# Attention into a top-1 mixture of experts: half of the first weights, the second layer's and two stores moved behind the gathered rows, plan steps spread over the next block

## The chip, the core and the metric

The kernel runs on one core of a Trainium2 chip. The core has five engines with queues of their own: TensorE (PE, products and transposes; PEld is its weight load), VectorE (DVE), ScalarE (ACT), GpSimd (POOL) and SyncE (SP, which here only issues DMAs). They wait for one another by semaphores. The metric is the device time of one execution in microseconds, as the median of several runs.

## The reference

Two stages. First a chunked attention: 4 batches, 8 heads, 768 positions, head size 64; each chunk of 32 positions sees 16 positions to its left, 8 to its right and 8 memory slots. Its output x has 3072 tokens of 512 numbers. Then each token goes to one of eight experts:

```python
logits = x @ w_gate + modality_bias[modality_id]
e_idx = np.argmax(logits, axis=1)
gate_w = probs[np.arange(N), e_idx]     # probs: softmax of the logits
for e in range(E):
    mask = e_idx == e
    h = np.maximum(x[mask] @ w1[e], 0.0)      # 512 -> 1024
    out[mask] = gate_w[mask, None] * (h @ w2[e])   # 1024 -> 512
```

All is in fp32; the kernel splits the expert products into a rounded high part and a low part (the difference), so that each product of the reference is three on TensorE.

## The kernel before, in words

**Attention.** 16 units (a batch and two heads), two halves each, in one long loop. After each unit its output (tile xb) is stored to a DRAM tensor xd, whose rows are tokens: 512 numbers of x and 16 copies of the gate. After each batch, route(b) computes the logits, the expert of each token, its place in the expert's list, and the gates; it is a generator whose steps third() and pump() put between other work. The list of tokens of each expert is a table of columns.

**Expert blocks.** Work then goes in slots, each with a block of up to 256 tokens of one expert. gather(row) reads the block's token numbers from the table (a column whose number stands in a register), and two indirect DMAs on GpSimd's queue fetch 128 rows of xd each into xg[0] and xg[1]. load_w(row, half) issues on SP eight loads of 256 KB: half 0 is the first layer (raw[0] to raw[7]), half 1 the second (raw[8] to raw[15]); they are skipped by a register if the block has the expert of the one before. cast makes the high parts on ScalarE; less makes the low parts on VectorE or GpSimd; conv is both. trans transposes the gathered rows and splits them (xt); mm1(f) makes one of eight pieces of the hidden layer (12 products), after which ScalarE and VectorE write its high and low part (h); mm2(f) makes the second layer's products for both halves of the tokens.

**The passage.** Block 0 is of the expert that is largest after three batches, and takes tokens of those alone. So its weights are loaded and its rows gathered while batch 3's attention ends, and mm1 and mm2 of block 0 run beside batch 3's routing. When that is done, plan_early finds block 1 (register regs1), and plan_rest, another generator, finds all the others (register regs). In the first slot (opening) plan_rest's steps stand between other work on VectorE, and what is left is run at its end; the slot after it begins with its loads and its gather, which need regs, and then the stores of block 0's results.

**What sets the order.** Each engine runs its instructions in program order, and so do SP's and GpSimd's DMA issues: a DMA that waits holds all that are behind it. A load into a buffer waits for the last reader of that buffer. In a slot, TensorE runs eight mm1 of the block, then mm2(0) to mm2(2), trans(0) of the next block, mm2(3), trans(1), and the rest of mm2. Results of transposes and of mm1 go through four buffers in turn (bank, named tr).

The functions that the diff touches, with the lines of the profile:

Of the kernel before, what the change touches and what calls it, by code (L numbers as in the profile page):

```python
# [20 lines left out]
P = 128  # L21
# [12 lines left out]
HEAD = 3  # L34
# [14 lines left out]
def tile_chunk_attention_top1_moe(  # L49
# [344 lines left out]
    def trans_x(u, hf):  # L394
        b, g = divmod(u, 4)
        xb = xbs[u]
        t = bank()
        for i in range(3):
            nc.tensor.transpose(t[:, i * P:(i + 1) * P], xb[:, 3 * hf + i, :], ident)
        if hf == 0:  # L400
            xTs[u] = rt.tile([P, S], F32, name="xT", bufs=5)
        nc.scalar.copy(xTs[u][:, 384 * hf:384 * hf + 384], t[:, 0:384])
        if hf == 1:
            (nc.sync if u in (NU - 4, NU - 3) else nc.gpsimd).dma_start(xd[b * S:(b + 1) * S, g * P:(g + 1) * P].rearrange("(t p) c -> p t c", p=P), xb)


    routing, now = [], [0]
# [165 lines left out]
    def route(b):  # L573
# [86 lines left out]
        yield "v"  # L660
        nc.vector.reciprocal(sx, sx)
        yield "v"
        gt = sm.tile([P, NT, XW - DM], F32, name="gt")
        nc.gpsimd.tensor_copy(gt, sx.to_broadcast([P, NT, XW - DM]))
        with nc.allow_non_contiguous_dma(reason="one gate per token"):
            (nc.sync if b == B - 2 else nc.gpsimd).dma_start(xd[b * S:(b + 1) * S, DM:XW].rearrange("(t p) c -> p t c", p=P), gt)
        if b == B - 2:

            nc.vector.reduce_max(cm, cb, axis=AX.X)
# [15 lines left out]
        for t in range(NT):  # L685
            if b != B - 2 or t not in early:
                yield from one_hot(b, t, lo, ac, hot)
        yield "late" if b < B - 1 else "pe"
        tb = bank()
        for t, (l1, a1) in enumerate(hot):  # L690
# [20 lines left out]
    gate_now, gate_out = [const.tile([P, 2], F32, name=f"gate_{i}") for i in range(2)]  # L711
    ev = {}

    def load_w(row, half):
        if half == 0:
            if row == 0:
                ev[0] = nc.values_load(regs0[0:1, 0:1], engines=[mybir.EngineType.SP], min_val=0, max_val=E - 1,
                                       skip_runtime_bounds_check_because="the place of one of 8 experts")
            else:
                r = (regs1 if row < 2 else regs)[row:row + 1]  # L720
                ev[row] = nc.values_load(r[:, 0:1], engines=[mybir.EngineType.SP], min_val=0, max_val=E - 1,
                                         skip_runtime_bounds_check_because="the place of one of 8 experts, or 0")
                ev[row, "c"] = nc.values_load(r[:, 1:2], engines=[mybir.EngineType.SP], min_val=0, max_val=1,
                                              skip_runtime_bounds_check_because="a comparison gives 0 or 1")
        e = ev[row]
        kw = {} if row == 0 or row == ROW_X and half == 0 else {"cond": ev[row, "c"]}
        for f in range(8):
            if half == 0 and row < ROW_X:
                nc.sync.dma_start(
                    raw[f].rearrange("p (c f) -> p c f", f=P),  # L730
                    w1[ds(e, 1), :, f * P:(f + 1) * P].rearrange("o (c p) f -> p (o c) f", p=P), **kw)
            elif half == 0:
                src = w1[ds(e, 1), :, (f // 4) * DM:(f // 4 + 1) * DM]
                c = f % 4
                nc.sync.dma_start(
                    raw1[32 * c:32 * c + 32, f - c:f - c + 4],
                    src[:, c * P:(c + 1) * P].rearrange("o (c s) f -> s (o c) f", s=32), **kw)
            else:
                nc.sync.dma_start(raw[8 + f], w2[ds(e, 1), f * P:(f + 1) * P, :].rearrange("o p d -> p (o d)"), **kw)
# [176 lines left out]
    for i in range(n + 1):  # L916
        live = i < n
        u, hf = units[i] if live else (NU, 0)
        now[0] = i
        if i == MAN:  # L920
            man.enter_context(tc.manual_schedule(engines={mybir.EngineType.Pool}))
        if i < n - 1:
            scores(u, hf)
        if 1 <= i < n - 1:
            exps_t(*units[i - 1])
        if i == n - 5:
            third(7)
        if i < n - 1:
            less_max(u, hf)
            if i == 1:  # L930
                nc.vector.memset(vws[1][0:64, :, D:2 * D], 0.0)
            pump(1)
        if u + 1 < NU and hf == 0:
            trans_k(u + 1)
            regroup_q(u + 1)
            pump(3)
            store_k(u + 1, 1, 0, nc.scalar.copy)
            store_k(u + 1, 0, 0, nc.scalar.copy)
            store_k(u + 1, 0, 1, nc.scalar.copy)
            store_k(u + 1, 1, 1, nc.scalar.copy)  # L940
            pump(3)
        elif u + 1 < NU:
            if u == 0:
                nc.gpsimd.iota(iota_i, [[1, 192]], base=0, channel_multiplier=0)
                mem_keys(2, nc.gpsimd)
            if 0 < u < NU - 2:
                mem_keys(u + 2, nc.gpsimd)
            if u + 1 < NU - 1:
                share_v(u + 1)
            trans_q(u + 1)  # L950
            store_q(u + 1, 0)
            store_q(u + 1, 1)
            pump(5)
        elif live:
            pump(5)
        if i == n - 3:
            third(5)
        if i == n - 2:
            scores(*units[i + 1])
        if i == n:  # L960
            attend(*units[i - 1])
        if i == n - 1:
            attend(*units[i - 1])
            exps_t(*units[i])
            cast(1)
        if 2 <= i <= n:
            trans_x(*units[i - 2])
        if i == n - 5:
            third(1)
        if i == n - 2:  # L970
            third(1)
            gather(0)
            less_max(*units[i + 1])
            exps_t(*units[i])
            cast(0)
        if 1 <= i < n - 1:
            attend(*units[i - 1])
        if i == n - 5:
            third(2)
            normalize(*units[i - 1])  # L980
            third(5)
        if i == n:
            less(0)
        if i >= 1 and i != n - 5:
            normalize(*units[i - 1])
            if i == 1:
                nc.vector.memset(vws[2][64:P, :, 0:D], 0.0)
            if i in (2, 3):
                c = NCH // 2 * (i - 2)
                nc.vector.memset(vws[2][0:64, c:c + NCH // 2, D:2 * D], 0.0)  # L990
            pump(1)
        if i == n - 6:
            third(3)
        if i == n - 5:
            third(1)
        if i == n - 4:
            share_v(NU - 1, range(2))
            third(8)
            share_v(NU - 1, range(2, 8))
        if 2 <= i < n:  # L1000
            u2, hf2 = units[i - 2]
            if hf2 == 1 and u2 % 4 == 3:
                routing.append((route(u2 // 4), True, u2 // 4, 0))
        if i == 4:
            routing.append((more_constants(), False, -1, 0))
        if i == 8:
            assert not routing
            bias_rows()
        if i < n:
            pump(1, True)  # L1010
        if live and hf == 0:
            if 0 < u < NU - 3:
                load_qk(u + 3)
            if u >= 1 and u - 1 + NVW < NU:
                load_v(u - 1 + NVW)
        if (u, hf) == (NU - 2, 1):
            c_ld.close()
            xp = ctx.enter_context(tc.tile_pool(name="xp", bufs=1, side="right"))
            ix = xp.tile([P, 2], I32, name="ix")
            gx = xp.tile([P, 2], I32, name="gx")  # L1020
            xg = [xp.tile([P, XW], F32, name=f"xg{t}", align_bytes=256) for t in range(2)]
            xth, xtl = [xp.tile([P, 4, 256 + NR], F32R, name=f"xt{i}") for i in range(2)]
            hh, hl = [xp.tile([P, 8, 256], F32R, name=f"h{i}") for i in range(2)]
            load_w(0, 0)
    third(3)
    assert not routing
    routing.append((route(B - 1), True, B - 1, 0))
# [33 lines left out]
    gate_q = [hp.tile([P, 1], F32, name=f"gate_q{i}") for i in range(2)]  # L1061
    out_q = out.rearrange("n (a d) -> (n a) d", d=P)
    load_w(0, 1)
    third(1)
    mm1(1)
    third(6)
    less(4)
    cast(6)
    cast(7)
# [61 lines left out]
        if f in (3, 4) and not whole:  # L1131
            turned(f - 3)

    def slot(row, rest=None, rest_next=None, opening=False):
        begin(row, opening, rest_next)
        if not opening:
            for f in range(8):
                mm1(f, rest is not None, row is not None and row <= ROW_X)
                conv(8 + f)
        if rest is None and row is not None:  # L1140
            load_w(row, 1)
        for f in range(6):
# [4 lines left out]
                load_w(row, 1)  # L1147
            if opening:
                conv(f)
                if f < 5:  # L1150
                    next(steps, None)
            elif row is not None:
                prepare(f, row < ROW_X)
# [36 lines left out]
    more = ExitStack()  # L1190
    steps = plan_rest()
    slot(1, opening=True)
    for _ in steps:
        pass
    for r in range(2, HEAD + 1):
        slot(r, rest_next=0 if r == HEAD else None)
    nextra, ntail = [
        nc.values_load(nsl[0:1, i:i + 1], min_val=0, max_val=m, skip_runtime_bounds_check_because="the tokens make no more")
        for i, m in ((0, NEXTRA), (1, NTAIL))
# [43 lines left out]
```

## Time and profile before

| | |
|---|---|
| median of 3 runs | 438.85 us (438.73 to 439.16) |
| the profiled execution | 440.44 us |
| its span in the trace | 438.6 us |
| PE busy | 413.9 us, 94% |
| DVE busy | 309.7 us, 71% |
| ACT busy | 272.2 us, 62% |
| POOL busy | 209.9 us, 48% |
| DMA | 69.30 MB, mean 158 GB/s |

Times in rows are microseconds from the start of the span; durations of groups are in ns where it says so. Busy says that an instruction ran, not that it was useful, and an engine that waits costs time only if the end of the program waits for it. The slices of the profile show TensorE busy nearly throughout but for the stretch from about 120 to 175 us, where attention passes into the expert blocks.

### The profile page before, as it was taken

The page shows a single profiled execution, that of the slowest core. Times are in us where ns is not written, and L with a number is a line of the kernel's source. Part 1 is how long each engine was busy: PE and PEld are TensorE (multiplying, and loading weights), DVE is VectorE, ACT ScalarE, POOL GpSimd, SP SyncE. Part 2 cuts the span into 40 slices and gives each one's busy share as a digit, 9 for nine tenths or more (in the row PEclk, how much of TensorE's full clock was granted, in tenths as well). Part 3 has the DMA queues.
Part 4 walks back from the last instruction along what each step waited for, and adds up shares of the span by engine and source line. Part 5 has one row for each costly group of instructions (what it writes and reads, how often), then busy time and mean ns, then how long its engine had stood idle before and what let it go on. Part 6 is the DMA issues. An engine that isn't in the chain of part 4 may idle for free. (4 is left out here: it accounts for less than half of the span.)

```text
span 438.6 us, 11888 instructions
## 1 busy us (share of the span) xinstructions
PE 413.9 (94%) x4053; PEld 354.7 (81%) x4053; DVE 309.7 (71%) x749; ACT 272.2 (62%) x545; POOL 209.9 (48%) x416
## 2 busy tenths in 40 slices
PE   7899999999976997999999999999999999999994
PEld 4687778887755876989898898989898988898983
DVE  6889797896983879957646466685859594858540
ACT  5878787878763844746456465666666564656531
POOL 7898889999973980561053404505032205320101
PEclk9999999999996998999999999999999999999999
DMA  6889998997398001286276977505597404340101
GB/s 195 215 214 240 275 221 219 272 249 185 102 245 302 7 17 35 88 253 198 55 214 195 260 213 245 169 27 164 120 244 245 141 4 149 100 143 1 48 2 48
DMA packets 80402, 69.30 MB, mean 158 GB/s; under 512 B 37531, under 2 KB 66867, under 8 KB 80324
## 3 DMA queue, kind: packets, MB, share of 16 engines
q1 hardware_dynamic: 73840, 49.68, 42.0%
q0 software_dynamic: 5632, 18.57, 13.3%
q8 instruction: 37, 0.61, 0.6%
q14 instruction: 41, 0.34, 0.3%
q10 hardware_dynamic: 852, 0.11, 0.2%
HBM read 81.25 MB, written 16.58 MB: 223 GB/s over the span
## 5 line engine op out<-in xcount | busy, mean ns | idle before, releaser
L825 PEld LDWEIGHTS tr<-xt,w 128*128 128x128 f32 x1152 | 140.4, 189 | 5.3 <-issue 1.8
L825 PE MATMUL tr<-xt,w 128*128 128x256 f32 (+1 forms) x1152 | 142.0, 284 | 2.1 <-DVE xt L784 1.0
L835 PE MATMUL av<-wh,h 128*128 128x512 f32 x384 | 125.7, 399 | 0.0
L829 DVE SCALAR_TENSOR_TENSOR h<-tr,h 128x256 fp32r<-128x256 f32 x96 | 40.6, 423 | 65.4 <-ACT h L826 47.7
L835 PEld LDWEIGHTS av<-wh,h 128*128 128x128 f32 x384 | 72.6, 189 | 16.6 <-issue 0.4
L835 PE MATMUL av<-wl,h 128*128 128x512 f32 x192 | 75.8, 395 | 0.0
L826 ACT ACTIVATE h<-tr 128x256 fp32r<-128x256 f32 x96 | 36.9, 384 | 54.2 <-PE tr L825 48.2
L296 POOL COPY vw<-vw 24x384 f32<-24x384 f32 (+1 forms) x128 | 65.8, 514 | 8.1 <-DMA vw<-in_v_dram 1.4
L860 POOL DMA_INDIRECT out_dram<-o,ix x24 | 25.3, 1053 | 92.7 <-ACT o L856 90.7
L750 DVE TENSOR_TENSOR wl<-raw,wh 128x512 fp32r<-128x512 f32 x90 | 62.5, 694 | 7.0 <-ACT wh L746 0.2
L750 DVE TENSOR_TENSOR w<-raw,w 128x512 fp32r<-128x512 f32 x92 | 59.1, 682 | 8.1 <-ACT w L746 5.6
L746 ACT CAST wh<-raw 128x512 fp32r<-128x512 f32 x96 | 58.8, 615 | 0.0
L746 ACT CAST w<-raw 128x512 fp32r<-128x512 f32 x96 | 52.9, 619 | 6.5 <-DMA raw<-in_moe_w_dram 6.5
L338 ACT COPY kbd<-tr 64x672 f32<-64x672 f32 x62 | 48.2, 778 | 5.3 <-PE tr L332 4.2
L835 PEld LDWEIGHTS av<-wl,h 128*128 128x128 f32 x192 | 36.4, 190 | 7.7
L856 ACT ACTIVATE o<-av,gate 128x512 f32<-128x512 f32 x24 | 16.3, 688 | 39.2 <-PE av L835 31.1
L768 POOL DMA_INDIRECT xg<-xd,gx x24 | 27.5, 1148 | 13.9 <-POOL gx L766 5.2
L346 PE MATMUL sc<-kbd,qT 128*32 128x128 f32 x768 | 27.3, 275 | 1.3 <-DVE kbd L338 1.3
L376 PE MATMUL av<-vw,PT 128*32 128x130 f32 x768 | 27.7, 278 | 0.8 <-ACT PT L366 0.7
L366 ACT ACTIVATE PT<-tr 128x384 f32<-128x384 f32 x32 | 15.8, 493 | 17.8 <-PE tr L364 17.7
L376 PEld LDWEIGHTS av<-vw,PT 128*32 128x32 f32 x768 | 19.3, 109 | 6.0 <-issue 3.7
L346 PEld LDWEIGHTS sc<-kbd,qT 128*32 128x32 f32 x768 | 20.4, 110 | 4.7 <-issue 3.4
(253 smaller groups left out, 523.1 us busy)
## 6 DMA issues: line engine op xcount, KB each, us to landing
raw<-in_moe_w_dram SPq DMA_DIRECT2D x192, 256.0 KB
k<-in_k_dram SPq DMA_DIRECT2D x16, 384.0 KB
q<-in_q_dram SPq DMA_DIRECT2D x16, 384.0 KB
vw<-in_v_dram SPq DMA_DIRECT2D x32, 184.0 KB
xd<-xb POOLq DMA_DIRECT2D x14, 384.0 KB, 5.3
xs<-xg SPq DMA_DIRECT2D x14, 256.0 KB
xq<-xs SPq DMA_DIRECT2D x28, 128.0 KB
vw<-in_mem_v_dram SPq DMA_DIRECT2D x32, 48.0 KB
```

The lines of the kernel that those rows point to most:

```text
L296: nc.gpsimd.tensor_copy(vw[r0:r0 + 24, c + 1:c + 1 + w, d], vw[r0 + 32:r0 + 56, c:c + w, d])
L338: copy(dst.rearrange("p c (i j) -> p c i j", j=2)[:, :, :, j], win)
L346: nc.tensor.matmul(sc[32 * j:32 * j + 32, t * P:(t + 1) * P], qT[:, 32 * c:32 * c + 32], kbd[:, c].rearrange("p h m -> p (h m)"), start=Tr ...
L376: nc.tensor.matmul(avb[32 * j:32 * j + 32, t * W:(t + 1) * W], PT[:, t * P + 32 * j:t * P + 32 * j + 32], vw[:, c, 0:W], start=True, stop= ...
L746: nc.scalar.copy(wh[i], raw[i])
L750: (eng or nc.vector).tensor_sub(wl[i][:, s], raw[i][:, s], wh[i][:, s].bitcast(F32))
L768: nc.gpsimd.indirect_dma_start(out=xg[t], out_offset=None, in_=xd[0:rows], in_offset=bass.IndirectOffsetOnAxis(ap=gx[:, t:t + 1], axis=0))
L825: nc.tensor.matmul(pw, wt[i][:, j * P:(j + 1) * P], x[:, c, 0:w], start=(n == 0), stop=(n == 11))
L826: nc.scalar.activation(hh[:, f], ph, AF.Relu)
L829: nc.vector.scalar_tensor_tensor(hl[:, f], ph, 0.0, hh[:, f].bitcast(F32), op0=ALU.max, op1=ALU.subtract)
L835: nc.tensor.matmul(pos[t], x, w[8 + f], start=(f == 0 and n == 0), stop=(f == 7 and n == 2))
L860: nc.gpsimd.indirect_dma_start(out=out, out_offset=bass.IndirectOffsetOnAxis(ap=to[:, t:t + 1], axis=0), in_=outs[t], in_offset=None, boun ...
```

## The change

Five edits. (1) load_w takes a list of pieces. SP issues only the first four loads of block 0's first layer where all eight stood. The other four are issued after the gather of block 0: a one-element copy on GpSimd from xg[1] into raw[4] makes load 4 wait until the gathered rows are there, and SP's later issues stand behind it. (2) The stores of the last two units' xb go from GpSimd's queue to SP's, behind these loads and ahead of the second layer's. (3) The gates of batch 3 are copied by ScalarE instead of GpSimd, after the third one-hot, and stored by SP behind the second layer's loads. (4) Before mm1(1), six more steps of the last routing stand ahead of VectorE's work on h(1). (5) In the opening slot plan_rest gives only three of its steps; the others run in the next slot (second=True), one after each of the first four mm1 and the rest after the fifth. That slot's loads and gather are issued after them, and the stores of block 0's results at its beginning.

```diff
-            (nc.sync if u in (NU - 4, NU - 3) else nc.gpsimd).dma_start(xd[...], xb)
+            (nc.sync if u >= NU - 4 else nc.gpsimd).dma_start(xd[...], xb)
...
+        def gates():
+            gt = sm.tile([P, NT, XW - DM], F32, name="gt")
+            (nc.gpsimd.tensor_copy if b < B - 1 else nc.scalar.copy)(gt, sx.to_broadcast([P, NT, XW - DM]))
+            with nc.allow_non_contiguous_dma(reason="one gate per token"):
+                (nc.sync if b >= B - 2 else nc.gpsimd).dma_start(xd[b * S:(b + 1) * S, DM:XW].rearrange("(t p) c -> p t c", p=P), gt)
+        if b < B - 1:
+            gates()
...
                 yield from one_hot(b, t, lo, ac, hot)
+            if b == B - 1 and t == 2:
+                gates()
...
-    def load_w(row, half):
+    def load_w(row, half, parts=range(8)):
...
             gather(0)
+            nc.gpsimd.tensor_copy(raw[4][0:1, 0:1], xg[1][0:1, DM:DM + 1])
+            load_w(0, 0, range(4, 8))
...
-            load_w(0, 0)
+            load_w(0, 0, range(4))
...
-    third(1)
+    third(7)
     mm1(1)
-    third(6)
...
-    def slot(row, rest=None, rest_next=None, opening=False):
-        begin(row, opening, rest_next)
+    def slot(row, rest=None, rest_next=None, opening=False, second=False):
+        if not second:
+            begin(row, opening, rest_next)
+        else:
+            keep(False)
+            for t in range(2):
+                finish(t, gate_out)
+            store(ix_out)
         if not opening:
             for f in range(8):
                 mm1(f, rest is not None, row is not None and row <= ROW_X)
                 conv(8 + f)
+                if second and f == 4:
+                    for _ in steps:
+                        pass
+                    load_w(row, 0)
+                    gather(row)
+                    if rest_next is not None:
+                        gather_rest(rest_next)
+                elif second and f < 4:
+                    next(steps, None)
...
-                if f < 5:
+                if f < 3:
                     next(steps, None)
...
     slot(1, opening=True)
-    for _ in steps:
-        pass
     for r in range(2, HEAD + 1):
-        slot(r, rest_next=0 if r == HEAD else None)
+        slot(r, rest_next=0 if r == HEAD else None, second=r == 2)
```

TensorE's order is the same in both kernels. What moves is shown for SP and VectorE.

SP at the passage, before: raw_90 are first-layer pieces, raw8 and raw9 second-layer ones; in brackets the semaphores that a row waits for (DMAHW of an earlier DMA, Pool of GpSimd).

```order
L729 DMA raw_90<-in_moe_w1_dram 128x4x128 [waits DMAHW4_49]
...
L729 DMA raw_90<-in_moe_w1_dram 128x4x128 [waits DMAHW5_49]
...
L729 DMA raw_90<-in_moe_w1_dram 128x4x128 [waits DMAHW0_49]
L739 ISA
L739 DMA raw8_2966<-in_moe_w2_dram 128x512 [waits PE_49,DMAHW1_49,Activation_49,Pool_49]
...
L739 DMA raw9_2969<-in_moe_w2_dram 128x512 [waits DMAHW2_49]
```

The same place after, with xb_2707 and xb_2848 the outputs of the last two units:

```order
L735 DMA raw_90<-in_moe_w1_dram 128x4x128 [waits DMAHW4_49]
...
L735 DMA raw_90<-in_moe_w1_dram 128x4x128 [waits DMAHW5_49,Pool_49]
...
L735 DMA raw_90<-in_moe_w1_dram 128x4x128 [waits DMAHW0_49]
L404 DMA xd_86<-xb_2707 128x6x128 [waits DMAHW1_49,DVE_49]
L404 DMA xd_86<-xb_2848 128x6x128 [waits DMAHW2_49,DVE_49]
L745 ISA
L745 DMA raw8_2967<-in_moe_w2_dram 128x512 [waits DMAHW3_49,PE_49,Activation_49]
```

The fifth load has a wait on GpSimd now, and two stores stand between the last first-layer load and raw8.

VectorE in the opening slot, before: w is a low part of the first layer, xt the low part of block 1's rows, the 64x8 rows are plan steps.

```order
L505 TENSOR_TENSOR end<-sta,free 64x8
L750 TENSOR_TENSOR w_190<-raw,w_189 128x512
L508 SCALAR_TENSOR_TENSOR cum<-tail 64x8
L509 TENSOR_TENSOR pt<-cum,tail 64x8
L510 TENSOR_SCALAR is_r_3397<-rowc,cum 64x1
L511 CAST nsl<-cum 1x1
L750 TENSOR_TENSOR w_190<-raw,w_189 128x512 x2
L784 TENSOR_TENSOR xt_2719<-tr,xt_2718 128x2x256 x2
L750 TENSOR_TENSOR w_190<-raw,w_189 128x512
L515 TENSOR_SCALAR isf<-sta,turn,rowc 64x8
```

After:

```order
L490 SCALAR_TENSOR_TENSOR col_3353<-first,has_3352 64x8
L756 TENSOR_TENSOR w_190<-raw,w_189 128x512 x4
L790 TENSOR_TENSOR xt_2719<-tr,xt_2718 128x2x256 x2
L756 TENSOR_TENSOR w_190<-raw,w_189 128x512
L835 SCALAR_TENSOR_TENSOR h_2721<-tr,h_2720 128x256
L756 TENSOR_TENSOR wl_2969<-raw_2967,wh_2968 128x512
L496 TENSOR_TENSOR own<-free,ohg 64x8
L497 TENSOR_TENSOR oth<-free,noth 64x8
```

Between col and xt stood four w with 13 plan steps (own to end, cum to nsl) among them; now the four w stand there alone, block 1's first h and wl come before own, and the plan goes on behind them.

VectorE where the plan ends and regs is written, before:

```order
L534 SCALAR_TENSOR_TENSOR four<-pick_3350,rowc,four 64x24
L538 SCALAR_TENSOR_TENSOR four<-col_3352,rowc,four 64x8
L540 TENSOR_REDUCE rows<-four 64x4
L541 CAST regs<-rows 64x4
L829 SCALAR_TENSOR_TENSOR h_2721<-tr,h_2720 128x256
L750 TENSOR_TENSOR wl_2968<-raw_2966,wh_2967 128x512
```

After, in the next slot; h and wl of mm1(4) are the first two rows, h of mm1(5) the last:

```order
L835 SCALAR_TENSOR_TENSOR h_2721<-tr,h_2720 128x256
L756 TENSOR_TENSOR wl_2981<-raw_2979,wh_2980 128x512
L530 TENSOR_TENSOR four<-isf,iota 64x8
L531 TENSOR_TENSOR c<-first,ist 64x8
L532 TENSOR_TENSOR four<-four,c 64x8
L534 SCALAR_TENSOR_TENSOR four<-pick_3328,is_r_3483,four 64x24
L536 TENSOR_SCALAR four<-col_3330,is_r_3483 64x8
L534 SCALAR_TENSOR_TENSOR four<-pick_3351,rowc,four 64x24
L538 SCALAR_TENSOR_TENSOR four<-col_3353,rowc,four 64x8
L540 TENSOR_REDUCE rows<-four 64x4
L541 CAST regs<-rows 64x4
L835 SCALAR_TENSOR_TENSOR h_2721<-tr,h_2720 128x256
```

Before, regs stood ahead of the first h of that slot; now five pairs of h and wl are ahead of it.

## Rows read from the trace of the kernel before

**Rows 1.** Waits of TensorE up to 195 us (total, times, longest).

```profile
PE tr L807 <- DMA xg<-xd,gx: 6.6, 4, 2.4
...
PE tr L622 <- DVE oh L611: 0.8, 1, 0.8
```

**Rows 2.** The same from 195 us to the end.

```profile
PE tr L825 <- PEq L1210: 0.6, 1, 0.6
```

**Rows 3.** TensorE in order of time: start, duration, instruction, idle before.

```profile
130.21 0.55 PE L399 MATMUL tr<-ident,xb 128*128 128x128 f32 x3
132.72 0.30 PE L807 MATMUL tr<-ident,xg 128*128 128x128 f32 x1 [1.96 <-DMA xg<-xd,gx]
135.44 1.75 PE L807 MATMUL tr<-ident,xg 128*128 128x128 f32 x7 [2.43 <-DMA xg<-xd,gx]
...
138.57 2.23 PE L825 MATMUL tr<-xt,w 128*128 128x256 f32 x12
...
167.01 1.71 PE L807 MATMUL tr<-ident,xg 128*128 128x128 f32 x7 [1.23 <-DMA xg<-xd,gx]
...
170.83 1.10 PE L825 MATMUL tr<-xt,w 128*128 128x256 f32 x8
172.92 11.07 PE L825 MATMUL tr<-xt,w 128*128 128x256 f32 x88 [0.98 <-DVE xt L784]
```

**Rows 4.** TensorE, later: block 2's first transposes, then its mm1.

```profile
188.04 0.60 PE L807 MATMUL tr<-ident,xg 128*128 128x128 f32 x4
...
195.86 11.38 PE L825 MATMUL tr<-xt,w 128*128 128x256 f32 x96
```

**Rows 5.** Second gather of blocks 0 to 3: count, us to landing.

```profile
xg<-xd,gx POOLq DMA_INDIRECT x1, 7.6
...
xg<-xd,gx POOLq DMA_INDIRECT x1, 3.6
...
xg<-xd,gx POOLq DMA_INDIRECT x1, 3.9
...
xg<-xd,gx POOLq DMA_INDIRECT x1, 6.4
```

**Rows 6.** GpSimd in order of time: second gathers of blocks 0 and 2, differences.

```profile
127.83 1.38 POOL L768 DMA_INDIRECT xg<-xd,gx  x1 [0.30 <-issue]
...
130.13 3.88 POOL L750 TENSOR_TENSOR w<-raw,w 128x128 fp32r<-128x128 f32 x8
...
180.73 1.49 POOL L768 DMA_INDIRECT xg<-xd,gx  x1 [0.30 <-issue]
```

**Rows 7.** Windows: length, engines' busy time, granted clock, DMA share, GB/s.

```profile
126.00:128.00 2.00, 1.87 (x39) 1.23 (x35) 1.86 (x7) 1.05 (x4) 1.28 (x2) 1.00 1.11 280
...
136.00:138.00 2.00, 2.00 (x14) 1.00 (x12) 0.84 (x2) 1.17 (x2) 0.00 (x0) 0.50 1.06 407
...
168.00:170.00 2.00, 2.00 (x8) 1.71 (x7) 1.90 (x14) 1.73 (x4) 0.00 (x0) 0.50 0.01 4
```

**Rows 8.** SP's issues of block 0's first layer.

```profile
122.30 5.43 SPq L729 DMA_DIRECT2D raw<-in_moe_w_dram  x8
```

**Rows 9.** ScalarE: casts of pieces 8 and 10, first one-hot step.

```profile
144.62 1.14 ACT L746 CAST wh<-raw 128x512 fp32r<-128x512 f32 x2
...
147.99 0.40 ACT L550 ACTIVATE dist<-iota,lo 128x128 f32<-128x128 f32 x1
```

**Rows 10.** VectorE: plan steps, and the first pair of block 1.

```profile
168.70 0.15 DVE L496 TENSOR_TENSOR own<-free,ohg 64x8 f32<-64x8 f32 x1
...
170.99 1.27 DVE L750 TENSOR_TENSOR w<-raw,w 128x512 fp32r<-128x512 f32 x2
...
177.50 0.16 DVE L541 CAST regs<-rows 64x4 int32<-64x4 f32 x1
177.58 0.41 DVE L829 SCALAR_TENSOR_TENSOR h<-tr,h 128x256 fp32r<-128x256 f32 x1
177.91 0.67 DVE L750 TENSOR_TENSOR wl<-raw,wh 128x512 fp32r<-128x512 f32 x1
178.51 0.41 DVE L829 SCALAR_TENSOR_TENSOR h<-tr,h 128x256 fp32r<-128x256 f32 x1
```

More of the change, by code (lines that the diff above doesn't have):

```diff
@@ L403, in trans_x @@
         if hf == 1:
-            (nc.sync if u in (NU - 4, NU - 3) else nc.gpsimd).dma_start(xd[b * S:(b + 1) * S, g * P:(g + 1) * P].rearrange("(t p) c -> p t c", p=P), xb)
+            (nc.sync if u >= NU - 4 else nc.gpsimd).dma_start(xd[b * S:(b + 1) * S, g * P:(g + 1) * P].rearrange("(t p) c -> p t c", p=P), xb)
     routing, now = [], [0]
@@ L662, in route @@
         yield "v"
[L663 to L666, printed above, removed]
+        def gates():
[5 more added lines that the diff above has]
+            gates()
         if b == B - 2:
@@ L712, in tile_chunk_attention_top1_moe @@
     ev = {}
-    def load_w(row, half):
-        if half == 0:
+    def load_w(row, half, parts=range(8)):
+        if half == 0 and parts[0] == 0:
             if row == 0:
@@ L726, in load_w @@
         kw = {} if row == 0 or row == ROW_X and half == 0 else {"cond": ev[row, "c"]}
-        for f in range(8):
+        for f in parts:
             if half == 0 and row < ROW_X:
```

## The prediction

> **What bounds the kernel now.** I read the waits of TensorE first. Before 195 us the gathered rows hold it longest, 6.6 us in four waits [rows 1]; after 195 us nothing holds it but two of its own branches, the longer 0.6 us [rows 2]. So from 195.86 us, where the third block's products start [rows 4], TensorE never stops, and what it gains or loses ahead of that goes to the end one for one, as long as weights arrive.
>
> Next, TensorE in order of time [rows 3]. The last transpose of attention ends at 130.76. One transpose of gathered rows runs at 132.72, when the first half of block 0 has landed, and seven from 135.44, when the second has. mm1(0) starts at 138.57. Block 1's gather holds it again until 167.01, and block 1's mm1(0) runs eight products from 170.83 and then waits for the low part of x until 172.92.
>
> Third, the landings [rows 5]: the second gather needs 7.6 us beside the first-layer weights, block 1's 3.6 with nothing beside it, block 2's 3.9, block 3's 6.4 beside block 3's weights. Fourth, the windows [rows 7]: the granted clock is 0.50 at 136 to 138 and at 168 to 170, the 1.2 GHz level; each time TensorE had just stood through both waits of a gather, with one transpose between them. Last, VectorE's order around 160 to 180 us [rows 10].
>
> **First part, at the gather.** SP issues the eight first-layer loads in 5.43 us [rows 8], 0.68 each, so four of them are issued by 125.0. They are 1.05 MB, at 280 GB/s [rows 7] 3.7 us, and through by about 127, before the second gather's issue at 127.83 [rows 6]. That gather then has nothing beside it: landing after 3.6 instead of 7.6 us, at 131.4 instead of 135.4, is 4.0 us sooner. If it flew as block 3's does it would be 6.4, only 1.2 us sooner; I take 3.6, since the bytes beside it are gone. TensorE then stands 0.7 us, not 4.4, and the clock should stay up: seven transposes take about 1.05 (four take 0.60 [rows 4]) instead of 1.75, and the twelve products of mm1(0) 1.4 (96 take 11.38) instead of 2.23. mm1(0) ends 5.5 us sooner.
>
> Six small VectorE steps of the last routing pass in front of h(1), so TensorE's 0.8 us wait for them [rows 1] goes too; up to here the chain is 6 us ahead.
>
> Now what is late next. GpSimd waits for the landing before its one-element copy, and its next differences queue behind it: two that mm1(1) and mm1(3) use, 1.94 us each (3.88 for eight quarters [rows 6]), so done about 133.7 and 135.7 and needed at 136.2 and 139.4. SP's second four loads queue behind that copy: first issue at about 132.0. Behind them stand the two stores, now on SP (0.9 us of GpSimd's time each is saved, off the path), and behind these the second layer. ScalarE casts pieces 8 and 10 at 144.62 now, and its eight one-hot steps start at 147.99 [rows 9]; VectorE's next h and with it the whole placing chain stand behind these. Six us ahead, ScalarE would ask for piece 8 at about 139.7. Worked out from a start of bytes 1 us after issue, 133.0: 1.05 MB of first layer at 280 GB/s is 3.7 us, 0.79 MB of stores 2.8, three second-layer pieces (0.79 MB) at 407 GB/s [rows 7] 1.9: piece 10 is there at 141.4, with some tenths for the completion at 141.8. Its cast ends at 142.4, and h(3), a cast and the one-hots follow: they start at 143.4, 4.6 us sooner than now. Bounds: no wait at all, 6.0; all 2.63 MB at 280 GB/s plus a slow start of the loads, 3.0.
>
> A page would move this a little: the Trainium skill, DMA: Bandwidth & Descriptors, section "Where 436 GB/s comes from", says that loads from HBM are held to about 358 GB/s per core. The 407 GB/s of the row stands above that, so here the row decides; by the page the three pieces would take 2.2 us, 0.3 more, and the gain would be 4.3.
>
> The gates: ScalarE's copy is at most one of its casts (0.57 us, two take 1.14 [rows 9]), at least nothing; VectorE's one-hots set the next h there, so I take nothing. Their store on SP goes when the second layer is issued, long before block 1 gathers. The chain from the one-hots to block 1's gather is VectorE's and moves as one, so block 1's rows land 4.6 us sooner. TensorE will wait longer for the last one-hot, some 3 us, but reaches the block 1 wait with that hidden: first part 4.6 us.
>
> **Second part, blocks 1 and 2**, told on the clock of the trace before, so 4.6 comes off at the end. Thirteen plan steps leave VectorE's queue ahead of the low part of x: they fill 168.70 to 170.99 [rows 10] but for one difference of 0.6, so 1.7 us. It is done that much sooner, TensorE's wait at 172.92 goes, and the eight mm1, 13.2 us from 170.83 to 183.99, shrink towards 11.4: 1.5 us gained at that point. Block 1 and block 2 have block 0's expert and move no weights (4 GB/s at 168 to 170 [rows 7]), so loads are no part of this.
>
> But the plan's end gives the register that block 2's gather needs. Now regs is written at 177.50, ahead of all eight h. After the change five pairs of h and difference stand ahead of it, at 0.93 us a pair (177.58 to 178.51 [rows 10]) 4.65, and VectorE stands about 0.7 for the first h. VectorE has no other pause there, so regs comes 5.4 us later, at 182.9. Everything behind it moves along: the second gather's issue from 180.73 [rows 6] to 186.1, its landing 3.9 us later [rows 5] from 184.6 to 190.0. TensorE transposes these rows at 188.04 now [rows 4], 3.4 us after they land. After the change it gets there at 186.5 and waits for 190.0. Against now that is 1.9 later; with 3.6 for the landing 1.6, and if the first h is no wait 1.2. The store moved ahead of this gather saves at most those tenths. I take 1.85.
>
> This stall has the shape of the one that ends at 167.01: a wait, one transpose, a second wait. After that one, seven transposes and six products took from 167.01 to 170.83, 3.8 us, where full speed is 2.05: 1.75 lost. After the first one the same loss was 0.7 and 0.8, 1.5. I add 1.75, since the same work follows; bounds 0 (the clock holds) and 1.75.
>
> Sum: 4.6 gained, 1.85 and 1.75 given back, 1.0 us net. The profiled execution, 440.44 with 1.84 us outside its span, would take 439.4; the median of the runs, 438.85, is 0.4% below it, and 1.0 off gives 437.8. The likeliest case's own range is 436.2 to 439.2.
>
> **The rivals.**
> Block 2's gather stays hidden. The first part stands, 1.5 us stays gained at the first block's products, nothing is given back: 6.1 off, 432.7. For it speaks only today's slack of 3.4 us; against it that VectorE's queue has no gap from which 5.4 us could come back. 0.12.
> The stall is there but the clock holds: 4.6 less 1.85, 436.1. For it: dense work, eight mm1 and three mm2, stands right ahead of this stall. Against it: mm2 of block 0 stood as densely ahead of the one that ends at 167.01, and the clock fell. 0.15.
> The second layer comes late and it gets slower. Piece 10 now stands behind 1.84 MB that were not all ahead of it, and ScalarE takes its casts in order, so every microsecond that it lands after 141.8 comes off the first gain. From 142.8 the change loses. If the loads start a microsecond later and flow at half of 407 GB/s, it lands near 145: gain 1.4, given back 3.6, 441.0. The even flow at 280 GB/s speaks against it. 0.13.
> The gather gains little. It lands after 6.4 us in spite of the held loads: 1.2 us sooner, 0.8 and 0.7 more if the clock still rises earlier, so about 1.5 to 2.5 off against 3.6: 440.4. Against it the 3.6 of block 1. 0.10.
>
> **How the numbers follow.** Forecast 0.50. Measurements of this kernel tell apart about 0.2%, 0.88 us. The forecast's centre lies just past that bound: I give 0.31 of its 0.50 to faster, 0.17 to same, 0.02 to slower. The first two rivals are faster, 0.27; of the last two, 0.23 in all, 0.07 falls within the bound and 0.16 beyond. So faster 0.58, same 0.24, slower 0.18. The range for 8 in 10 runs from the hidden case's near side, 433.0, to 440.4, and leaves out about 0.18.
>
> **What would show it.** Right: the first gathers land within 4 us; no clock of 0.50 at the first mm1; ScalarE waits for a second-layer weight by about a microsecond; regs of the plan stands after the fifth h; TensorE waits 3 us or more for block 2's rows and its clock falls behind that. Wrong: block 2's transposes start without a wait (then 433), or ScalarE stands several microseconds for piece 10 (then 440 and over).

## The result, and the profile after

The changed kernel takes 441.95 us as the median of 21 runs (440.15 to 443.54); the kernel before, run beside it, 439.62 (437.76 to 442.12). The ratio is 1.0051 [1.0038, 1.0063]: slower by 2.2 us, where 1.0 us less was forecast, and outside the range. The profiled execution of after took 441.2 us, with a span of 439.4.

TensorE in order of time, after (start, duration, instruction, in brackets the idle time before it and what ended it):

```profile
130.61 0.27 PE L813 MATMUL tr<-ident,xg 128*128 128x128 f32 x1
131.14 0.98 PE L813 MATMUL tr<-ident,xg 128*128 128x128 f32 x7 [0.25 <-DMA xg<-xd,gx]
...
133.05 1.70 PE L831 MATMUL tr<-xt,w 128*128 128x256 f32 x12
...
162.42 0.99 PE L813 MATMUL tr<-ident,xg 128*128 128x128 f32 x7 [0.85 <-DMA xg<-xd,gx]
...
164.65 1.11 PE L831 MATMUL tr<-xt,w 128*128 128x256 f32 x8
166.66 11.08 PE L831 MATMUL tr<-xt,w 128*128 128x256 f32 x88 [0.90 <-DVE xt L790]
...
183.52 0.30 PE L813 MATMUL tr<-ident,xg 128*128 128x128 f32 x1 [1.56 <-DMA xg<-xd,gx]
187.36 0.90 PE L813 MATMUL tr<-ident,xg 128*128 128x128 f32 x3 [3.53 <-DMA xg<-xd,gx]
190.62 1.05 PE L813 MATMUL tr<-ident,xg 128*128 128x128 f32 x4
...
197.23 2.97 PE L831 MATMUL tr<-xt,w 128*128 128x256 f32 x24
```

Set it beside [rows 3, 4]. Attention's last transpose ends at 130.8 in both. Block 0's rows now make TensorE wait 0.25 us, where it stood 1.96 and 2.43. Block 1's seven transposes start at 162.42, not 167.01: 4.6 us ahead, as forecast. Block 1's 88 products start 6.3 us ahead. Then all of that is lost at block 2: TensorE waits 1.56 and 3.53 us for its rows, which stopped nothing before, and block 2's mm1 starts at 197.23, not 195.86.

ScalarE at the passage, after, to be read with [rows 9]:

```profile
141.10 0.62 ACT L752 CAST wh<-raw 128x512 fp32r<-128x512 f32 x1 [2.23 <-DMA raw<-in_moe_w_dram]
142.33 0.62 ACT L752 CAST wh<-raw 128x512 fp32r<-128x512 f32 x1 [0.61 <-DMA raw<-in_moe_w_dram]
...
143.64 0.41 ACT L550 ACTIVATE dist<-iota,lo 128x128 f32<-128x128 f32 x1
```

It waits for second-layer pieces, 2.8 us in all where about one was expected, and its one-hots start at 143.64 (143.4 forecast). So the passage went as predicted. Now GpSimd at block 2's gather, after:

```profile
180.13 1.04 POOL L774 DMA_INDIRECT xg<-xd,gx  x1 [0.52 <-POOL gx L772]
181.48 3.50 POOL L774 DMA_INDIRECT xg<-xd,gx  x1 [0.30 <-issue]
184.99 0.19 POOL L760 COPY ix<-ix 128x2 int32<-128x2 int32 x1
```

and VectorE at the same place:

```profile
178.18 0.16 DVE L541 CAST regs<-rows 64x4 int32<-64x4 f32 x1
178.25 0.41 DVE L835 SCALAR_TENSOR_TENSOR h<-tr,h 128x256 fp32r<-128x256 f32 x1
...
181.05 3.08 DVE L756 TENSOR_TENSOR w<-raw,w 128x512 fp32r<-128x512 f32 x5
```

regs is written at 178.18 and the second gather begins to issue at 181.48; the prediction's 182.9 and 186.1, less its 4.6, are 178.3 and 181.5. But issuing took 3.50 us, where 1.49 stood before [rows 6], and it lasted from just inside VectorE's five differences (181.05 to 184.13) until 0.85 us after them. TensorE's clock, in the windows of after (length, busy times, granted clock third from the end, DMA share, GB/s):

```profile
184.00:186.00 2.00, 0.00 (x0) 0.00 (x0) 0.14 (x1) 0.00 (x0) 1.54 (x5) 0.75 0.19 34
186.00:188.00 2.00, 0.64 (x4) 0.65 (x4) 0.00 (x0) 0.00 (x0) 0.35 (x2) 0.50 0.27 101
188.00:190.00 2.00, 2.00 (x7) 1.61 (x6) 1.09 (x2) 1.10 (x2) 0.23 (x2) 0.50 0.64 185
```

It falls to 0.50, the 1.2 GHz level, while TensorE stands, and is still there at 190, in the work behind the stall.

### The profile page after: what moved, and what is told of

Its sections match the earlier page's. It is cut to its first block, busy times and chain, and to the rows that moved or that the text cites. A ratio compares the mean times of both kernels' runs of the same rounds, so it can differ in the third digit from the quotient of the medians.

```text
span 439.4 us, 11890 instructions
## 1 busy us (share of the span) xinstructions
PE 413.2 (94%) x4053; PEld 354.7 (81%) x4053; DVE 308.7 (70%) x749; ACT 272.1 (62%) x546; POOL 206.3 (47%) x413
## 5 line engine op out<-in xcount | busy, mean ns | idle before, releaser
L841 PE MATMUL av<-wh,h 128*128 128x512 f32 x384 | 127.1, 403 | 0.0
L841 PEld LDWEIGHTS av<-wh,h 128*128 128x128 f32 x384 | 73.5, 191 | 17.0 <-issue 0.4
L296 POOL COPY vw<-vw 24x384 f32<-24x384 f32 (+1 forms) x128 | 64.9, 507 | 7.9 <-DMA vw<-in_v_dram 1.2
L774 POOL DMA_INDIRECT xg<-xd,gx x24 | 28.7, 1194 | 15.8 <-POOL gx L772 4.9
```

The source lines that it names most:

```text
L296: nc.gpsimd.tensor_copy(vw[r0:r0 + 24, c + 1:c + 1 + w, d], vw[r0 + 32:r0 + 56, c:c + w, d])
L774: nc.gpsimd.indirect_dma_start(out=xg[t], out_offset=None, in_=xd[0:rows], in_offset=bass.IndirectOffsetOnAxis(ap=gx[:, t:t + 1], axis=0))
L841: nc.tensor.matmul(pos[t], x, w[8 + f], start=(f == 0 and n == 0), stop=(f == 7 and n == 2))
```

## The experiments

The theory after this result: the give-back at block 2 is larger than thought, because GpSimd's issue of the second gather is held while VectorE makes five differences with two SBUF inputs each. Rivals: the landing itself is slower; the first part gained less than it seems; VectorE's mere business holds GpSimd. Ratios are to the kernel before, run on the same chip beside each; gains and losses in us are worked out from them.

**First part alone.** After, with the plan as before (dots within a line stand for an argument).

```diff
-                if f < 3:
+                if f < 5:
...
+    for _ in steps:
+        pass
...
-        slot(r, ..., second=r == 2)
+        slot(r, ..., second=False)
```

> The changed kernel with the plan's steps put back where they were (five in the opening slot, the rest at its end, block 2's loads and gather at the head of the next slot): the passage alone is changed. Theory: the passage gains what the trace after shows at block 1's rows, 4.1 to 4.6 us, and nothing downstream takes it back, so the time is 4.0 to 4.6 us below before (ratio about 0.990) and block 2's rows land before TensorE asks for them, with no wait of TensorE after block 1's first product. Rival: the early gather is paid back later anyway (loads, stores or the clock at block 2), and the time is within 1 us of before.

Measured: 436.67 us where before is 440.4, ratio 0.992 [0.9889, 0.995]. TensorE:

```profile
164.57 1.11 PE L831 MATMUL tr<-xt,w 128*128 128x256 f32 x8
168.30 12.58 PE L831 MATMUL tr<-xt,w 128*128 128x256 f32 x88 [2.61 <-DVE xt L790]
...
184.93 0.60 PE L813 MATMUL tr<-ident,xg 128*128 128x128 f32 x4
...
192.75 11.38 PE L831 MATMUL tr<-xt,w 128*128 128x256 f32 x96
```

A window behind the wait:

```profile
170.00:172.00 2.00, 2.00 (x11) 2.00 (x11) 1.72 (x14) 0.44 (x1) 0.00 (x0) 0.50 0.00 0
```

The first part wins 3.5 us, less than the 4.0 to 4.6 expected. Block 1's 88 products start 4.6 us sooner than before (168.30 against 172.92), as forecast. But TensorE comes to the low part of x sooner than VectorE, which still has the plan's steps ahead of it, and waits 2.61 us; behind that wait the granted clock is 0.50, the 88 products take 12.58 us where they took 11.07 [rows 3], and at block 2's mm1 3.1 us are left (192.75 against 195.86). Block 2's rows are there without a wait.

**Plan spread alone.** Before, with only the second part, edit (5) of the change; its main lines:

```diff
-                if f < 5:
+                if f < 3:
...
+                if second and f == 4:
+                    for _ in steps:
+                        pass
+                    load_w(row, 0)
+                    gather(row)
```

> The kernel before with the plan's spread alone (three steps in the opening slot, the rest after mm1(0) to mm1(4) of the next, loads and gather of block 2 behind them, stores first). Theory with GpSimd held: block 2's second gather is issued while VectorE runs its five differences in a row, takes 3 us or more to issue instead of 1.5, and with the stall and the low clock the kernel is 5 to 6 us slower than before. Rival, the size in the prediction: the issue takes 1.5 us, the rows land 5.4 us later than now, and it is 3.6 us slower (1.85 of stall, 1.75 of clock).

Measured: 445.7 us, ratio 1.0121 [1.0086, 1.0155], 5.3 us more. The second gather on GpSimd:

```profile
185.91 3.52 POOL L768 DMA_INDIRECT xg<-xd,gx  x1 [0.30 <-issue]
```

The five differences:

```profile
185.49 3.08 DVE L750 TENSOR_TENSOR w<-raw,w 128x512 fp32r<-128x512 f32 x5
```

The issue is held in the same way without the first part: from inside the five to 0.86 us behind them. The spread by itself loses; the 3.6 us of my own terms fall short by about what the issue lasts longer.

**Differences later.** After, with the five differences of block 2's weights moved behind its first xt.

```diff
-            conv(i)
+            (cast if late and f < 3 else conv)(i)
...
+        if late and f == 2:
+            for i in range(5):
+                less(i)
```

> The changed kernel with one move: the five differences that VectorE runs in a row ahead of block 2's first xt are run right after it instead; all else, the late register too, is the same. Theory with GpSimd held by VectorE: the second gather's issue falls from 3.5 to about 1.0 to 1.5 us, its rows land 1.8 to 2.2 us sooner, and the kernel is about 2 us faster than the changed one, 0 to 0.5 us above before. Rival, the issue is held by something else (the DMA queue behind the stores, or the gather's own descriptors): the issue stays near 3.5 us and the time stays at the changed kernel's, 2.2 us above before.

Measured: 439.06 us, ratio 0.9978 [0.9954, 1.0001], some 3.2 us below the changed kernel, where about 2 was expected. GpSimd:

```profile
182.59 0.97 POOL L774 DMA_INDIRECT xg<-xd,gx  x1 [0.30 <-issue]
```

TensorE:

```profile
163.49 1.04 PE L813 MATMUL tr<-ident,xg 128*128 128x128 f32 x7 [1.06 <-DMA xg<-xd,gx]
...
166.89 11.94 PE L831 MATMUL tr<-xt,w 128*128 128x256 f32 x96
...
184.76 0.30 PE L813 MATMUL tr<-ident,xg 128*128 128x128 f32 x1 [1.72 <-DMA xg<-xd,gx]
186.15 0.55 PE L813 MATMUL tr<-ident,xg 128*128 128x128 f32 x3 [1.08 <-DMA xg<-xd,gx]
```

Its clock, at block 1's rows and behind the waits for block 2's:

```profile
164.00:166.00 2.00, 2.00 (x9) 1.65 (x8) 1.97 (x11) 1.93 (x4) 0.00 (x0) 0.57 0.03 8
...
186.00:188.00 2.00, 1.85 (x10) 1.53 (x11) 0.65 (x2) 1.11 (x2) 0.58 (x3) 1.00 0.00 0
```

Nothing of the gather was touched, only VectorE's order, and the issue went from 3.50 to 0.97 and the two waits from 5.1 to 2.8. What is more than expected is the clock's: it is 1.00 behind these waits. The wait that is left I put down to the plan's place. VectorE stood idle here, so this run does not yet tell a port from mere business.

**Rest of the plan after the second mm1.** After, with `f == 4` made 1.

```diff
-                if second and f == 4:
+                if second and f == 1:
...
-                elif second and f < 4:
+                elif second and f < 1:
```

> The changed kernel with the rest of the plan run after mm1(1) instead of mm1(4), so two pairs of h and difference stand ahead of the register instead of five. Theory: the register comes 2.8 us sooner than in the changed kernel, the second gather is issued beside pairs and not beside the five differences, its rows land about 4.8 us sooner, TensorE's wait of 5.1 us at block 2 shrinks to under 1 us and the clock stays up: 6 us faster than the changed kernel, 3.5 to 4.5 us faster than before. Rival: TensorE runs out of buffers for mm1 because VectorE's h(2) comes late, and half of that is lost: 2 us faster than before.

Measured: 435.99 us, ratio 0.9903 [0.9871, 0.9935]: 4.3 us less than before, the lowest ratio of all. TensorE:

```profile
177.01 3.11 PE L831 MATMUL tr<-xt,w 128*128 128x256 f32 x24 [1.18 <-DVE h L835]
184.17 0.60 PE L813 MATMUL tr<-ident,xg 128*128 128x128 f32 x4
```

The rows land in time, for a wait of 1.18 us at a buffer that h holds behind the plan. GpSimd in the same run:

```profile
179.77 1.42 POOL L774 DMA_INDIRECT xg<-xd,gx  x1 [0.30 <-issue]
181.20 0.19 POOL L760 COPY ix<-ix 128x2 int32<-128x2 int32 x1
181.33 0.18 POOL L761 COPY gate<-gate 128x2 f32<-128x2 f32 x1
181.46 3.82 POOL L762 COPY ix<-ix 128x2 int32<-128x2 int32 x1
```

VectorE's differences:

```profile
182.14 3.09 DVE L756 TENSOR_TENSOR w<-raw,w 128x512 fp32r<-128x512 f32 x5
```

Now the gather is out before them, and a copy of two numbers a partition is held instead: 3.82 us in place of 0.19, to 185.28, just after the last difference ends at 185.23. TensorE doesn't wait for that copy. Such a copy isn't always held so long. In the kernel before, two of them run beside the same five differences:

```profile
185.68 3.09 DVE L750 TENSOR_TENSOR w<-raw,w 128x512 fp32r<-128x512 f32 x5
...
187.56 0.66 POOL L755 COPY gate<-gate 128x2 f32<-128x2 f32 x1
188.15 0.66 POOL L756 COPY ix<-ix 128x2 int32<-128x2 int32 x1
```

They take 0.66 us each, about the length of one difference, and the first is through at 188.22, inside the five.

**The hold alone.** Before, with four of block 0's loads held behind the gathered rows (load_w takes its list of pieces as in the change) and nothing else.

```diff
             gather(0)
+            nc.gpsimd.tensor_copy(raw[4][0:1, 0:1], xg[1][0:1, DM:DM + 1])
+            load_w(0, 0, range(4, 8))
...
-            load_w(0, 0)
+            load_w(0, 0, range(4))
```

> The kernel before with only the hold: four first-layer loads at first, the other four behind the gathered rows by the one-element copy; stores, gates and plan as before. Theory (the hold is the gain of the first part): the second gather lands after about 4 us in place of 7.6, no 0.50 clock at the first mm1, and 3.0 to 3.9 us less than before, nearly all of the 3.7 that the whole first part gave. Rival (the steps of routing that stand ahead of mm1(1), and the stores and gates moved to SP, carry a good part): at most 2 us less.

Measured: 436.44 us where before is 440.08, ratio 0.9929 [0.9905, 0.9952], 3.1 us less. TensorE:

```profile
131.61 0.99 PE L807 MATMUL tr<-ident,xg 128*128 128x128 f32 x7 [0.41 <-DMA xg<-xd,gx]
...
168.26 11.00 PE L825 MATMUL tr<-xt,w 128*128 128x256 f32 x88 [2.50 <-DVE xt L784]
```

The seven transposes of block 0 start at 131.61 after 0.41 us of waiting.

**The first part without the hold.** The reverse: all eight loads at once, the rest of the first part kept, the plan as before.

```diff
-            nc.gpsimd.tensor_copy(raw[4][0:1, 0:1], xg[1][0:1, DM:DM + 1])
-            load_w(0, 0, range(4, 8))
...
-            load_w(0, 0, range(4))
+            load_w(0, 0)
```

> The first part without its hold: all eight first-layer loads at once as before, but stores and gates on SP and the six routing steps ahead of mm1(1); the plan as before. Theory (the hold is the gain): the second gather lands after 7 us or more, TensorE stands 4 us for it and its clock falls to 0.50; the time is within 1 us of before. Rival (the other edits gain by themselves): 2 to 3 us less than before.

Measured: 439.09 us, ratio 0.9983 [0.9962, 1.0005]. TensorE:

```profile
132.43 0.30 PE L813 MATMUL tr<-ident,xg 128*128 128x128 f32 x1 [1.46 <-DMA xg<-xd,gx]
134.54 1.75 PE L813 MATMUL tr<-ident,xg 128*128 128x128 f32 x7 [1.81 <-DMA xg<-xd,gx]
```

The two runs agree: the hold is nearly all of the first part's gain (0.71% with it alone, 0.17% and not told from nothing without it). That the edits of stores, gates and routing steps count is not shown. The second gather landed 7.0 us after its issue (127.51 to 134.54) beside all the loads, and 3.9 with four of them held (127.70 to 131.61). TensorE stood 3.3 us for the rows here, where 4 were expected.

**One SBUF input.** After, with the five differences replaced by a maximum over the same numbers, which leaves out the renewal of five low parts.

```diff
-            conv(i)
+            if one and i < 5:
+                cast(i)
+                nc.vector.reduce_max(peak, raw[i], axis=AX.X)
+            else:
+                conv(i)
```

> The changed kernel with the five differences in the third block's preparation (two SBUF inputs each) replaced by a maximum over the same 128x512 numbers (one SBUF input, a column out); the low parts of five weight pieces are not renewed there. Theory (a VectorE operation with two SBUF inputs holds up GpSimd's descriptor writing): the second indirect DMA of block 2 issues in about 1.0 us in place of 3.50 though VectorE is as busy, TensorE waits under 3 us for the rows, the clock stays at 1.00, and the time is 2.5 to 3.5 us less than the changed kernel, about 439 where before is 440. Rival (any VectorE work without a gap holds GpSimd): the issue stays at 3 us or more and the time at the changed kernel's, 0.5% above before.

Measured: 439.24 us, ratio 0.9979 [0.9961, 0.9997]. VectorE:

```profile
182.64 3.55 DVE L1138 TENSOR_REDUCE peak<-raw 128x1 f32<-128x512 f32 x5
```

GpSimd:

```profile
183.06 0.98 POOL L774 DMA_INDIRECT xg<-xd,gx  x1 [0.30 <-issue]
```

TensorE:

```profile
185.21 0.30 PE L813 MATMUL tr<-ident,xg 128*128 128x128 f32 x1 [1.69 <-DMA xg<-xd,gx]
186.61 0.55 PE L813 MATMUL tr<-ident,xg 128*128 128x128 f32 x3 [1.09 <-DMA xg<-xd,gx]
```

Its clock:

```profile
186.00:188.00 2.00, 1.39 (x7) 1.14 (x8) 0.39 (x2) 0.81 (x2) 0.58 (x3) 0.84 0.02 8
188.00:190.00 2.00, 2.00 (x9) 1.60 (x7) 1.10 (x2) 0.29 (x1) 0.00 (x0) 0.50 0.05 8
```

VectorE is as full as before over the whole issue (3.55 us from 182.64), and the issue takes 0.98. So it is not VectorE's business that holds GpSimd but the kind of operation; of the differences' second input and their wide output, both gone here, the run doesn't say which. Issue, waits and time are as expected; that the clock would stay up was a miss.

**Both cures.** After, with the rest of the plan after the third mm1 and the five differences late.

```diff
-                if second and f == 4:
+                if second and f == 2:
...
-                elif second and f < 4:
+                elif second and f < 2:
```

(and the edit of "Differences later")

> The changed kernel with the rest of the plan after the third mm1 of the second block (not the fifth) and the five differences moved behind block 2's first xt. Theory: the buffer wait of 1.2 us that came with the rest of the plan after the second mm1 goes, both issues take 1.0 us, and the gather comes about a microsecond later than there, so TensorE waits 0.5 to 1.5 us for block 2's rows instead: 3.5 to 4.5 us less than before, no better than the rest of the plan after the second mm1 (4.3 less). Rival: the two waits don't trade, both are gone: 5 us or more less than before.

Measured: 436.13 us, ratio 0.9922 [0.9892, 0.9951]. TensorE:

```profile
177.44 1.70 PE L831 MATMUL tr<-xt,w 128*128 128x256 f32 x12 [0.69 <-DVE h L835]
...
183.99 0.55 PE L813 MATMUL tr<-ident,xg 128*128 128x128 f32 x3 [0.52 <-DMA xg<-xd,gx]
```

The buffer wait shrinks from 1.18 to 0.69 and comes back as 0.52 for the rows. Of the issues one took 1.04, but the second 1.42 (expected 1.0), beside pairs of h and difference. No better than the rest of the plan after the second mm1, as expected: the two can't be told apart.

## Why the prediction was wrong

**The first part was right**: the second gather of block 0 lands 3.84 us after its issue (127.30 to 131.14; 3.6 taken), the first mm1 runs at full clock (twelve products in 1.70), ScalarE's one-hots start at 143.64 (143.4), block 1's rows are 4.59 us sooner (4.6). That the hold does it is shown by the two runs with and without it. On the way there ScalarE stood 2.8 us for second-layer pieces, not about one, and piece 10 was there at 142.33, not 141.8: no row gave the 1 us from issue to the first bytes that was put into that sum. The one-hots came 0.7 us behind that cast where 1.0 was taken, so part of their agreement is luck.

**Up to block 1's end the sum was right, and one wait in it was not.** 4.6 and 1.5 make 6.1 us; the 88 products start 6.26 sooner (166.66 against 172.92). In both kernels they start when VectorE has the low part of x, and the plan's steps that left its queue account for 1.64 of it (168.30 with them, in the first part alone). But the wait for xt did not go (0.90 us): TensorE came sooner too, since its clock no longer fell at block 1's rows, 2.23 us from the seven transposes to the first mm1, where it was 3.82. Where the clock did fall there, in "Differences later" (3.40 us), the wait is gone, as forecast.

**The place of regs was right, 178.18 against 178.3, and the step that failed is the next one**: "its landing 3.9 us later [rows 5] from 184.6 to 190.0". That took the time from issue to landing as a fixed number. It holds two things: GpSimd's issue, the time of its own instruction, and the flight behind it. The flight was the same, 2.4 us (before 180.73 and 1.49, landing 184.6; after 181.48 and 3.50, 187.36). The issue was not. The later gather fell in among VectorE's five differences, and these held it for 2.0 us more. So the rows came at 187.4, not 185.4, and TensorE stood 5.1 us, not 3.5. That the differences do it is shown: the plan alone has the same 3.52, the differences elsewhere give 0.97, a reduction with one SBUF input at the same place 0.98. The row that could have warned was 1.49 for an issue beside pairs of h and difference [rows 6], where 0.97 is the time beside an idle VectorE; I copied it and didn't ask what it would be beside five differences without a gap.

The clock's part was taken as 1.75; from the transposes to block 2's mm1 it is 9.87 us against 7.82 [rows 4], so 2.05. The 1.75 itself was read a little high: the work that it called 2.05 us at full speed took 2.23 in after at a clock of 1.00, so 1.6 had been lost there. Put together from the forecast of 1.0 us gained: 2.0 for the issue and 0.3 for the clock make 1.3 us lost, and block 2's mm1 is 1.37 late. The runs say 2.2. The rest of that is not traced; the profiled execution of before lies 0.8 us above the median of its runs, that of after 0.8 below, and single executions here differ by more.

The Trainium skill has a page on this that I did not weigh: SBUF — State Buffer, section "Who interferes with whom". It says that a VectorE instruction with two SBUF inputs contends with a GpSimd instruction that reads SBUF, and, of VectorE's two-port modes, that whoever issues first has the shared pair of ports for the whole instruction. The copies of 0.66 us in before fit a wait for one instruction; the copy of 3.82 us did not get in between five differences that follow each other without a gap, and no run shows why. The section also says that in a probe `tensor_tensor` did not stall DMAs, and infers that it leaves descriptor writing alone. Here the runs speak against it, 3.50 and 3.52 against 0.97 and 0.98. The gather takes its row numbers from a tile in SBUF, which may be why it is held; no run here shows which part of its work waits.

Of the rivals none came: block 2's gather was not hidden, the clock did not hold, the second layer came in time, and the first gather gained all. The truth was the likeliest case with two of its terms larger. The range gave block 2's landing no upper bound beyond the 3.9, although that transfer's surroundings were changed; 6.4 [rows 5] was there as the far row, and 2.5 us more makes 1.5 us lost, the right side, if less than the 2.2 measured.

## What to carry to other kernels

The time from issue to landing of a DMA that GpSimd issues is not a constant: split it into the issue, which five of VectorE's differences of two SBUF tiles in a row stretched from about 1.0 to 3.5 us here, and the flight. When a step is moved, look at what the other engine does at its new place, not only at what stands ahead of it in its own queue. And when a change has a part that gains and one that loses, time them apart: here the hold alone gains 0.7%, and with the rest of the plan three mm1 sooner the whole gains 1.0%. Whether the spread adds anything to the first part is not shown: 0.9903 with it at its best place and 0.992 without it can't be told apart.

## What the hardware showed that was not expected

A stall of the same shape does not always cost the clock. Block 2's waits of 1.72 and 1.08 us (differences later) were followed by a clock of 1.00, those of 1.69 and 1.09 (one SBUF input) by 0.84 and 0.50, with TensorE's order the same ahead of and behind both; from the three transposes to block 2's mm1 it was 7.77 us in the one and 9.39 in the other. At block 1's rows likewise: after waits of 0.95 and 1.19 us seven transposes took 0.98 (the hold alone), after 0.81 and 1.21 they took 1.74 (without the hold). A wait of 2.50 us for xt left 88 products at 11.00 us (the hold alone), one of 2.61 made them 12.58 (first part alone). The clock's past was not the same in the first two pairs: in "Differences later" it had fallen at block 1's rows (0.57), in "One SBUF input" it had not, and without the hold it had fallen at block 0's rows, with the hold alone not. Each is one execution, and the times of the first pair are alike (0.9978 and 0.9979). What decides stays open; to forecast the loss from one earlier stall, as I did, is a guess between 0 and 2 us.
